# Spacing loads and transposes with small GpSimd reads, and moving reciprocals and row fetches, in an attention + gated-MLP kernel

## The chip, the cores and the metric

One core of one Trainium2 chip. The metric is device time in microseconds (us) of one launch, taken over several runs. Four compute engines matter: TensorE (PE in the profile), VectorE (DVE), ScalarE (ACT) and GpSimd (POOL). In these kernels SyncE (SP) only issues transfers.

## The reference

Shortened:

```python
B, N, m, C = 4, 12416, 32, 128
scale = 1.0 / np.sqrt(C)
def mab(q, kv):                       # attention without projections
    s = scale * (q @ kv.transpose(0, 2, 1))
    a = np.exp(s - s.max(-1, keepdims=True))
    a /= a.sum(-1, keepdims=True) + 1e-09
    return a @ kv
h = mab(inducing, x)                  # 32 rows per batch: needs ALL of x of that batch
y = mab(x, h).reshape(B * N, C)       # 49664 tokens
gate = 1 / (1 + np.exp(-(y @ w_gate)))          # 128 -> 1536
out = (gate * (y @ w_val)) @ w_out              # 1536 -> 128
```

`h` of a batch needs the whole batch, so the kernel computes `h` of batch b+1 while it runs the MLP of batch b. The inputs arrive in float32 and the kernel works in float16.

## The kernel before

The MLP runs in 97 blocks of 512 tokens, 24 to a batch. A block has 12 chunks of 128 hidden units. ScalarE makes `T = tanh(gate/2)` from TensorE's product; VectorE makes `u = (T + 1) * value`; TensorE multiplies `u` with `w_out`. In some "shared" blocks GpSimd makes 3 of the 12 products, from a copy of the value that ScalarE leaves in SBUF, to relieve VectorE:

```python
SHARED = (3, 7, 11, 15, 19, 23)                  # of 24 blocks, from block 5 on
def v_mul_pool(v32, bi, j0, n):
    ...
        nc.gpsimd.tensor_tensor(out=t[:], in0=v, in1=Ts[...], op=ALU.mult)
        nc.gpsimd.tensor_tensor(out=u[:, jj, :], in0=t[:], in1=v, op=ALU.add)
```

All engines run in a written order. `PLAN` is a string of 97 words, one per block: `A` and `B` are VectorE's products of two and of one chunk, `G`/`W` ScalarE's, small letters the products with `w_out`, and `J` takes the next side job (pieces of the next batch's attention). Each `A` starts one of four steps, and `at(n, k, f)` emits `f` at step k of block n. A shared block has no step 0, so what is due there comes with step 1.

The token rows of the second attention (`rep`) are made for eight blocks at a time, by a chain that starts at block n:

```python
def rep_events(n, b, d):
    put(n, 1, "s2", b, d)                # scores, exp
    at(n + 1, 0, e2_dma, b, d)           # small transpose, SyncE
    at(n + 1, 3, s2_sum, b, d)           # row sums: a tree of five adds, GpSimd
    at(n + 2, 3, s2_rec, b, d)           # reciprocal, VectorE
    at(n + 2, 3, a2_mul, b, d, 0)        # normalise, GpSimd
    at(n + 2, 3, a2_mul, b, d, 1)
    at(n + 3, 0, a2_dma, b, d, 0)        # transpose back, SyncE
    at(n + 3, 1, a2_dma, b, d, 1)
    at(n + 3, 2, rep_put, b, d, 0)       # to a DRAM scratch
    at(n + 3, 3, rep_put, b, d, 1)
    at(n + 4, 0, rep_get, b, d, 0)       # fetch of the new rows, four replicas
    at(n + 4, 1, rep_get, b, d, 1)
```

The next batch comes in six quarters of 512 KB each (`load_x`, issued by GpSimd; the code calls them q, 0 to 5). Each is transposed by a big transfer (`xT_dma`, SyncE), scored (`s1`), its weights are transposed by a small transfer (`a1_dma`), and they multiply the rows (`h`):

```python
for b in range(B):
    n0 = b * BB                          # BB = 24
    rep_events(n0 + 2, b, 1); rep_events(n0 + 10, b, 2)
    ...
        if b == 0:
            loads = ((1, 0), (2, 0), (5, 0), (6, 0), (8, 0), (9, 0))
            s1s, s1t, fin = (5, 9, 12), 6, 16
            hs = ((8, 1), (9, 1), (12, 2), (13, 1), (14, 3), (15, 1))
        else:
            loads = ((-10, 0), (-7, 0), (-4, 0), (-1, 0), (2, 0), (5, 0))
            ...
        for q, ((ln, lk), (hn, hk)) in enumerate(zip(loads, hs)):
            at(n0 + ln, lk, load_x, nb, q)
            at(n0 + ln + 1, 2, xT_dma, nb, q)
            put(n0 + hn, hk, "h", nb, q)
        ...
        rep_events(n0 + fin + 2, nb, 0)
```

The softmax here doesn't subtract the row's maximum and nothing guards it: scores larger than these inputs give would overflow.

## Time and profile before

| | us |
|---|---|
| three runs | 705.4, 706.2, 712.2 |
| profiled run | 715.1 (counted slow; span 713.3) |
| VectorE busy / idle of the span | 666.2 / 47.1 |
| ScalarE busy, TensorE busy, GpSimd busy | 662.5, 679.8, 309.6 |

The profiled run is over 1% longer than most runs, so it shows more stalls than the typical one; it is read for what the stalls are, not for how long the kernel takes.

Table of 20-us windows of the kernel before. Columns: stretch, its length, then busy us of TensorE, its weight loads, VectorE, ScalarE and GpSimd (with counts), granted TensorE clock, transfer engines' busy share, GB/s.

```profile
60.00:80.00 20.00, 19.52 (x114) 6.38 (x112) 19.99 (x24) 19.80 (x25) 11.43 (x15) 1.00 0.93 140
80.00:100.00 20.00, 16.35 (x97) 4.92 (x95) 13.62 (x17) 13.51 (x16) 4.60 (x6) 0.83 1.16 135
100.00:120.00 20.00, 14.15 (x97) 4.27 (x94) 12.24 (x15) 11.97 (x15) 3.80 (x5) 0.83 1.23 146
120.00:140.00 20.00, 19.91 (x142) 6.69 (x135) 19.86 (x25) 19.92 (x24) 12.76 (x17) 1.00 0.92 148
```

The first and last line are the normal state: VectorE and ScalarE both full (19.86 to 19.99 and 19.80 to 19.92 of 20 us), so that a hole in VectorE is lost time. The middle two lines are the two stalls, 14.1 us of VectorE idle, with the granted clock at 0.83 on average: in each of them it stood at half for 6.8 us.

The chain that ended last, before, in order of time (start, us, what): the three transfers that make up most of the stalls.

```profile
72.21 7.99 DMA a2T_1_1_1204<-a_0_1_1_1149
...
81.07 3.56 DMA rep_1_1278<-dt_1_0_1230
...
97.39 13.17 DMA xT_154<-xq_3_1283
```

The first two belong to the chain of `rep` for block 8; the third is a big transpose, which ran beside the load of quarter 4 (issued at 87.5 us, landed at 106.0).

### The profile page before, as it was taken

Reading aid. Unit: us, or ns where it says so; the run is one execution under the profiler, and the core shown is the slowest. Engines: PE = TensorE matmul, PEld = TensorE weight load, DVE = VectorE, ACT = ScalarE, POOL = GpSimd, SP = SyncE. Lnnn points to the kernel's source line nnn. Section 1 sums busy time; section 2 is a strip of 40 time slices with the busy share of each in tenths; the row PEclk is TensorE's granted clock in tenths of the full one; section 3 lists DMA queues with packets and bytes.
Section 4 is the critical chain, followed back from the end, with each engine's and each line's share of the span. In section 5 each row is a group of like instructions: output and inputs, shape, how many; then the busy total and the mean of one; then the engine's idle time right before and its main releaser. Section 6 shows DMA issues by size and latency. Waiting matters only on the chain.

```text
span 713.3 us, 13070 instructions
## 1 busy us (share of the span) xinstructions
PE 679.8 (95%) x4561; PEld 238.2 (33%) x4561; DVE 666.2 (93%) x792; ACT 662.5 (93%) x773; POOL 309.6 (43%) x389
## 2 busy tenths in 40 slices
PE   7899788999999999999999999999999999999997
PEld 4433222333333323333333333333333333333334
DVE  2599686999999999999999999999999999999997
ACT  4699776999999999999999999999999999999995
POOL 5234504452643541743541651634723534633423
PEclk9999898999999999999999999999999999999999
DMA  9599999884888792397688584454192353263222
GB/s 177 95 110 158 183 71 187 139 184 84 145 188 130 125 209 60 90 183 135 106 187 148 111 164 103 94 142 77 39 169 67 60 149 80 60 150 74 60 53 75
DMA packets 163955, 85.95 MB, mean 120 GB/s; under 512 B 133392, under 2 KB 148144, under 8 KB 163888
## 3 DMA queue, kind: packets, MB, share of 16 engines
q1 hardware_dynamic: 143904, 45.95, 38.2%
q0 software_dynamic: 19696, 39.03, 27.1%
q8 instruction: 35, 0.57, 0.4%
q14 instruction: 32, 0.26, 0.2%
q10 hardware_dynamic: 288, 0.13, 0.1%
HBM read 39.34 MB, written 28.31 MB: 95 GB/s over the span
## 4 chain that ended last, share of the span: by engine, by line
PE 64%; ACT 10%; DVE 9%; DMA 8%; issue 4%; POOL 3%; SPq 1%; DVEq 0%; ACTq 0%; POOLq 0%
DMA xq_4_132<-in_x_dram 2%; DMA xT_154<-xq_3_1283 2%; DMA a2T_1_1_1204<-a_0_1_1_1149 1%; SPq L397 1%; DMA a1n_2_3819<-e_2_2_3703 1%; DMA on_7763<-oT_7761 1%; DMA a1n_2_6256<-e_3_2_6162 1%; DMA on_5277<-oT_5275 1%; PE acc_1687 L538 1%; DMA rep_1_1278<-dt_1_0_1230 0%; PE acc_4267 L538 0%; PE acc_2641 L538 0%; PE acc_1770 L538 0%; PE acc_5765 L538 0%; PE acc_3334 L538 0%
## 5 line engine op out<-in xcount | busy, mean ns | idle before, releaser
L538 PEld LDWEIGHTS <-wo_117 128*128 128x128 f16 x1152 | 94.2, 98 | 147.7 <-issue 93.8
L428 PEld LDWEIGHTS <-hw_165 32*128 32x128 f16 x466 | 19.1, 91 | 59.9 <-issue 54.5
L428 PEld LDWEIGHTS <-hw_168 32*128 32x128 f16 x456 | 19.8, 91 | 56.2 <-issue 53.9
L428 PEld LDWEIGHTS <-hw_167 32*128 32x128 f16 x464 | 19.4, 91 | 54.1 <-issue 51.2
L428 PEld LDWEIGHTS <-hw_166 32*128 32x128 f16 x468 | 19.4, 91 | 52.4 <-issue 49.8
L428 PEld LDWEIGHTS <-hwp_172 128*128 128x128 f16 x120 | 11.7, 97 | 14.3 <-issue 4.7
L428 PEld LDWEIGHTS <-hwp_169 128*128 128x128 f16 x110 | 10.7, 98 | 15.8 <-issue 8.6
L428 PEld LDWEIGHTS <-hwp_171 128*128 128x128 f16 x112 | 10.9, 97 | 13.7 <-issue 5.8
L428 PEld LDWEIGHTS <-hwp_170 128*128 128x128 f16 x108 | 10.5, 97 | 14.6 <-issue 7.3
L566 POOL DMA_DIRECT2D out_dram<-on_1411 x1 | 0.5, 532 | 21.3 <-DMA on_1411<-oT_1409 21.3
L245 PEld LDWEIGHTS <-ones 128*128 128x128 f16 x96 | 6.9, 97 | 8.1 <-DMA a1n_2_6256<-e_3_2_6162 2.1
L190 PE MATMUL warm<-ones 128*128 128x512 f16 x16 | 5.6, 530 | 1.5 <-DVE ones L140 1.5
L767 PE MATMUL s_1_1657<-xT_154,indT 128*32 128x512 f16 x8 | 1.2, 605 | 5.8 <-DMA xT_154<-xq_2_1174 4.2
L495 DVE SCALAR_TENSOR_TENSOR u_8_1670<-T_4_1559,vb_2_1668 128x512 f16<-128x512 f16 x1 | 0.7, 690 | 6.4 <-PE vb_2_1668 L428 6.4
L214 ACT ACTIVATE e_1_2_1666<-s_1_1657 128x1024 f16<-128x1024 f32 x1 | 1.0, 1024 | 5.9 <-PE s_1_1657 L767 5.9
L310 POOL COPY hwp_169<-hw_165 32x128 f16<-32x128 f16 x2 | 0.6, 282 | 12.9 <-ACT hw_165 L303 12.8
L239 ACT ACTIVATE a1nt_205<-s1t_203 128x32 f16<-128x32 f32 x1 | 0.2, 198 | 6.0 <-PE s1t_203 L235 6.0
L495 DVE SCALAR_TENSOR_TENSOR u_4_1402<-T_2_1358,va_1_1399 128x1024 f16<-128x1024 f16 x1 | 1.2, 1222 | 4.2 <-PE va_1_1399 L428 4.2
L566 POOL DMA_DIRECT2D out_dram<-on_888 x1 | 0.5, 537 | 10.5 <-DMA on_888<-oT_886 10.5
L508 POOL TENSOR_TENSOR vt_0_6656<-v_59_2_6653,T_0_6643 128x512 f32<-128x512 f32 x1 | 1.1, 1150 | 8.3 <-PE s_2_6670 L324 8.3
L551 ACT ACTIVATE o_10374<-acc_10278 128x256 f32<-128x256 f32 x2 | 0.8, 384 | 4.3 <-PE acc_10278 L528 3.8
L482 ACT ACTIVATE T_0_1397<-g_0_1394 128x1024 f16<-128x1024 f32 x1 | 1.0, 1024 | 3.9 <-PE va_1_1399 L428 3.9
(4281 smaller groups left out, 2802.5 us busy)
## 6 DMA issues: line engine op xcount, KB each, us to landing
xq_0_120<-in_x_dram POOLq DMA_DIRECT2D x1, 512.0 KB, 5.1
xq_1_122<-in_x_dram POOLq DMA_DIRECT2D x1, 512.0 KB, 6.9
xq_2_128<-in_x_dram POOLq DMA_DIRECT2D x1, 512.0 KB, 8.3
xq_3_130<-in_x_dram POOLq DMA_DIRECT2D x1, 512.0 KB, 10.2
xq_4_132<-in_x_dram POOLq DMA_DIRECT2D x1, 512.0 KB, 13.4
xq_5_134<-in_x_dram POOLq DMA_DIRECT2D x2, 256.0 KB, 14.1
xq_0_770<-in_x_dram POOLq DMA_DIRECT2D x1, 512.0 KB, 6.2
xq_1_875<-in_x_dram POOLq DMA_DIRECT2D x1, 512.0 KB, 10.1
```

The lines of the kernel that those rows point to most:

```text
L190: nc.tensor.matmul(ps[:, 0:TOK], ones[:, 0:P], ones[:], start=True, stop=True)
L214: nc.scalar.activation(out=e1[:, 0:w], in_=ps[:, 0:w], func=AF.Exp, scale=SCALE)
L245: nc.tensor.matmul(ps[:, cs:cs + P], ones[:, 0:P], a1n[(b, q)][:, j, :], start=first and j == 0, stop=last and j == 3,)
L397: nc.sync.dma_start(rep[g * M:(g + 1) * M, 4 * i:4 * i + 4].rearrange("m r j t -> m r (j t)"), dt[:].rearrange("(r m) t -> m r t", m=M),)
L428: nc.tensor.matmul(ps[:, ds(col, TOK)], weights(k["b"]), rep[rows, 4 * k["i"] + k["r"]], start=True, stop=True,)
L482: nc.scalar.activation(out=Ts[(bi, p)][:, :, 0:T], in_=ps[:].rearrange("p (a t) -> p a t", a=2)[:, :, 0:T], func=AF.Tanh, scale=0.5,)
L495: nc.vector.scalar_tensor_tensor(out=u[:, :, 0:T], in0=Ts[(bi, j0 // 2)][:, j0 % 2:j0 % 2 + n, 0:T], scalar=1.0, in1=ps[:].rearrange("p (a ...
L508: nc.gpsimd.tensor_tensor(out=t[:], in0=v, in1=Ts[(bi, j0 // 2)][:, j0 % 2 + jj, :], op=ALU.mult)
L538: nc.tensor.matmul(accs[bi][:, 0:T], wo16[:, j, :], u, start=(c == 0), stop=(c == NJ - 1))
L551: nc.scalar.activation(out=o32[:, h:h + w, :].rearrange("p b c -> p (b c)"), in_=accs[bi][:, ds(h * P, w * P)], func=AF.Copy, scale=0.5,)
L566: nc.gpsimd.dma_start(out[ds(row0, QT)].rearrange("(p j) c -> p j c", j=QT // P)[:, 4 * k["r"]:4 * k["r"] + 4, :], on[:],)
L767: nc.tensor.matmul(ps[r * M:(r + 1) * M, ts(i, TOK)], indT[:], xTs[a[0]][:, ds(q * QT + r * TOK, TOK)], start=True, stop=True,)
```

## The change

Intent: a load and a big transpose should not be in flight together. A small GpSimd copy reads two columns of the transposed quarter q-1, so it waits for that transpose; it stands ahead of the load of quarter q. The loads of batch 1 are spread out, the chain of `rep` starts a block earlier with its later parts moved, stores come about half a block later, and the whole `PLAN` is redrawn for the new places.

```diff
 PLAN = (
-    "GAGBWGAabGBcGAfeGBdGAhBWgJ AGilkjBGGAabcBGAfGBedGAhGgBiG ...
+    "GAGBWGAabGBcGAfeGBdGAhBWgJG AilkjBGAJaBbGAcGBfeGAdWBhgG ...
     [all 97 words redrawn, cut]
+    def load_fence(b, q):
+        t = smp.tile([P, 2], F16, tag="fence", name=f"fence_{b}_{q}")
+        nc.gpsimd.tensor_copy(out=t[:], in_=xTs[b][:, ds(q * QT, 2)])
     def rep_events(n, b, d):
         put(n, 1, "s2", b, d)
         at(n + 1, 0, e2_dma, b, d)
-        at(n + 1, 3, s2_sum, b, d)
-        at(n + 2, 3, s2_rec, b, d)
-        [a2_mul at (n+2, 3); a2_dma at (n+3, 0) and (n+3, 1);
-         rep_put at (n+3, 2) and (n+3, 3); rep_get at (n+4, 0) and (n+4, 1), cut]
+        at(n + 2, 0, s2_sum, b, d)
+        at(n + 3, 0, s2_rec, b, d)
+        for i in range(2):
+            at(n + 3, 0, a2_mul, b, d, i)
+            at(n + 3, 1, a2_dma, b, d, i)
+            at(n + 3, 3, rep_put, b, d, i)
+            at(n + 4, 2, rep_get, b, d, i)
...
-        rep_events(n0 + 2, b, 1)
-        rep_events(n0 + 10, b, 2)
+        rep_events(n0 + 1, b, 1)
+        rep_events(n0 + 9, b, 2)
...
-                loads = ((1, 0), (2, 0), (5, 0), (6, 0), (8, 0), (9, 0))
-                s1s, s1t, fin = (5, 9, 12), 6, 16
-                hs = ((8, 1), (9, 1), (12, 2), (13, 1), (14, 3), (15, 1))
+                loads = ((0, 3), (2, 2), (4, 1), (6, 0), (7, 3), (9, 2))
+                s1s, s1t, fin = ((5, 1), (9, 0), (12, 1)), 6, 15
+                hs = ((7, 1), (7, 3), (11, 1), (11, 3), (14, 1), (14, 3))
+                wait = 4
+                [wait = 6 for the later batches, cut]
...
+                if q:
+                    at(n0 + ln, lk, load_fence, nb, q - 1)
                 at(n0 + ln, lk, load_x, nb, q)
-                at(n0 + ln + 1, 2, xT_dma, nb, q)
+                at(n0 + ln + (lk + wait) // 4, (lk + wait) % 4, xT_dma, nb, q)
...
-                at(n0 + sn + 1, 1, a1_dma, nb, [2 * e, 2 * e + 1])
+                at(n0 + sn + 1, 0, a1_dma, nb, [2 * e, 2 * e + 1])
...
-        if stores and (done_out[n] == 10 or n >= NBK - 2):
+        while stores and (n >= NBK - 2 or len(stores) > 1 and done_out[n] == 4):
             stores.popleft()()
```

More of the change, by code (lines that the diff above doesn't have):

```diff
@@ L25 @@
 PLAN = (
-    "GAGBWGAabGBcGAfeGBdGAhBWgJ AGilkjBGGAabcBGAfGBedGAhGgBiG AlkjBGGAbacBGAfWBedGAhJBgG "
-    "AilkjBGGAabcBGAfWBedGAhGgBiG AlkjBGGAbaBcWAGfeBGdAGBhGg AGilkBjGAJBabcAGefBGdAGhgBGi "
-    "AGlBkjJAGBaGbAGcGBefGAdhGBgG AikljBGGAbBaefGAdGBchG AgGBikGAljBJAGaBGbcGAGfBedG "
-    "AhGgBiGAlJBkGAjJBGAGbacBfeG AGdhBgiAGlkjBGGAbBJaAGcfBGe AGdhBGgAGiBkljGAGBabef "
-    "AGdBJcGAhgBGikAGljJBGAGbaBcfG AGedBGgAGhBilGAGkjBJAGBaGbcG AefGBdGAhgGBiGAkljBJAGbaGBcf "
-    "AGeGdBhGAgiWBlGAkjJBG AGabfBecGAGdBghGAikGBlJjAGBaGbcG AfGBedGAhJBgGAilkjBGGAabBcefG "
@@ L32 @@
-    "AdGBghGAilkjBGGAbaBGcGAfBJe AGdhBGgAGilBkjGAGBabef AGdcBGgGAhiBkljGAGBbacfAGedgGBhG "
-    "AilkjBGGAbacBWAGfBedGAhGgBiG AlkjBGGAbacBJAGfBGeAGdghBG AGilBkjGAGBbafeAGdcGBG "
-    "AghBGiAGklBJjAGGBbacfAGedBGg AGhiBGkAGljBJAGBGabcGAeGfBdG AgGhBiGAlGkBjGAJbaBcAGfeBGdh "
-    "AGgiGBkGAljBJAGbGBGa AGBefdGAGchBgGAiGBlkjGAGBabce AGfBJdAGhgBWiAGkBljGAGBbacf "
-    "AGedGBghAGilkjBGGAabBGcAGefBGd AGhgBGiAGlkjBJGABbGafG AedGBcGAhgBWiGAklBjJGAaGbBcG "
-    "AfeGBdGAhJBgGAilkjBGGAbacBfe AGdgGBhGAilkjBGGAaBJbAGceBGf AGdhBGgAGilkBjGAGBabef "
@@ L38 @@
-    "AGdcGBgGAhiBGkAGljBJAGBGbaceG AGfBdghGAiWBklGAjJBGAGabcBfG AGedBhGAgGBGAGilkJjBGAaGbBGcf "
-    "AGedBWhAGgilBkjGAJaBbG AceGBfGAdhBWgGAilBkjGAJbBaG AcfGBeGAdBWghAGilkBjGGAabBceG "
-    "AfGdBgGAhiBGGAlkjBGGAbacGBe AGfdBhGAGgilBkjAGGBbafe AGcdBGhAGgiBlkjGAGBabceAGfdBgG "
-    "AGhikBljGAGBabcGAefBGdAGhgBGi AGlBkjGAGaBbcGAJBfeGAdGBhgG AilkjBGGAabfBedGAcGBhgG "
-    "AikljBJGAbGBacGAfWBedAGhgGBiG AlkGBGAjBJAGbBGacGAfGBedG AhGgBiGAlGkBjGAGBbacfAGeBJd "
-    "AGghBGiAGlkjBJGABbaGfG AedBchGGAgiBkljGAGBabceGAfBdGgh AGikljBGAJBbaGAcWBfeGAdGhBgG "
@@ L44 @@
-    "AilkjBGAGabBcGAeGBGAGfdBGh AGgikBGAGlBjJAGBbGae AGfdBGhGAgciBGAGlkBjJGABbGacG "
-    "AfGeBdGAhgWBiGAkljBJAGbacBfG AeGBdGAhJBgGAilkjBGGAbacBfGG AedBghiGAlkjBGGAbaBfedG "
-    "AGhBgciAGlkBjJGAaBbGcfAGedWBhgG AiGlBkGAjJBGAGabBcWAGfBedG AGhgBiGAlGkBjJAGBbaGGcAGfBJe "
-    "AGdBGhgGAilkBjGAGbBafeG AdcGBgGAhiGBkGAljBJGAbacBfG AeGBdhGAgGiBlGAkjBWGAabBcefG "
-    "AdGBghGAilkjBGGAbacBfeGAGBdGh AGgilBkjGAGBefbaAGdgBWh AGicBkljGAGBbacGAefdBGAGghBiG "
-    "AGlkjBGAGBbacGAfeBWdAGhgBGi AGlBkjGAGBabcGAefGBdGAhGBgiG AkljBGGAfeBbadGAhWBgcG "
@@ L50 @@
-    "AilkBjGGAabBcGAfeGBdGAhgBGiG AlkBjGGAbaBcAGfWBedGAhgGBiG AlkjBJAGbacBGAfGeBGAdWBhgG "
-    "AikljBGGAfedBabGAGhBgiG AclkjBGGAabcBGAGfBedGAhWgBiG AGlkBjGAGBbacAGefBWAGdhgBG "
-    "AGiBlkjGAGBabcAGefBdJAGGhBgG AikGlBjGAGBabfeAGdgBWh AGciBkljGAGBabcGAefBGdAGhgiBG "
-    "AGkljBGAGBbacGAfeBWdGAhgBGi AGlBkjGAGBabcGAefGBdGAJBhgG AilkjBGGAfeBbadGAGhgBcG "
-    "AilBkjGGAabBcGAfBGedGAhgWiBG AlkjBGGAbacBGAGfeBdGAGBhgiG AlkjBGGAabcBGAGfeBdGAGBGhg "
-    "AGiBlkjGAGBefabAGdhBWgG AicBlkjGAGBbacGAefBGdAGhgBGi AGlkBjGAGBbacGAefBWdGAhgBGi "
@@ L56 @@
-    "AGlBkjGAGBbacGAefGBdGAhGgBiG AlkjBGGAfebBadGAgWBhcG AikBljGGAabBcGAfeGBdGAhGBgiG "
-    "AlkBjGGAbBacAGfBWedAGhgBGiG AlkBjGAGbaBcGAefBGdGAhGgBiG AlkjBGGAbafBeGAdWBhgG "
-    "AcikBljGABaGbAcfeBdAhgBilkj"
+    "GAGBWGAabGBcGAfeGBdGAhBWgJG AilkjBGAJaBbGAcGBfeGAdWBhgG AilkBjGGAbaBcGAfeGBdGAhgGBiG "
+    "AlkBjGGAbBacGAfWBedGAhGBgiG AlkjBGGAbaBWcAGfeBGdAGhBgG AGilBkjGAJaBbcAGfeBGdAGhgBGi "
+    "AGlkBjJAGBGabAGcGBefGAdhGBgG AikBJGAlBGjJAGBGbac AGefBGdGAhgBWiAGlkjBGAGBbace "
+    "AGfdBhGGAgilBkjGAJaBbcAGeBJfG AdgBGhAGilBkjGAGBabcfAGeGdBhG AgiJBGAGklBjJAGBWabeG "
@@ new lines @@
+    "AfdGBchGAgiGBkljAGBWabcAGefBJ AGdhBgGAGilBkjGAGBbacfAGedBGg AGhiBGlAGkjBJGABaGbGAGceBJ "
+    "AGBfGdgGAhiGBlJkjAGBGabfG AedBGcGAgBJhAGilkjBGGAbaBcfG AeGdBhGAgJBiGAlkjBWGAabcBeG "
+    "AGfBdhGAgGiBlGAkBGjGAGBabcf AGedBGhAGgikBljGAGBabefd AGhgGBcGAilkjBGGAabcBefGAdGBhgG "
+    "AikljBGGAbacBGAfWBedGAhgGBiG AlkjBGGAbacBJAGBfedGAGhBGg AGilkBjGAGBbafeAGdgWBhG "
+    "AicBGAGklBJjGAGBabcfGAedGBgG AhiBJAGkljBJGABaGbcGAfGBedG AghGBiGAlkBjGGAbaBcfGAGBeGd "
+    "AGhgiBkGAGljBJAGBWfeb AGaBGdhgAGicGBlGAkjBWGAabBcfG AeGBdgGAhJBiGAlkjBWGAabcBeG "
@@ new lines @@
+    "AGfdBhGAgGBilGAkGBjGAGBbacf AGedBGhgAGiBkljGGAbBaefG AdhGBgGAciGBlkAGjJBGAGabBcJ "
+    "AGBJefGAdhGBgGAilkjBGAJaBbG AcGfeBGAdGgBGhAGilBkjAGGBabcG AeGfBdGAghGBiGAlkBjWG "
+    "AfebBGadAGhgiBcGAGlkBjJAGBbGac AGfeGBdGAhgBGiAGkljBJGABaGbcG "
+    "AfedBhGGAgilBkjJAGBbacGGefAGdhBGg AGilkBjGAJaBbGAfWBed AGchGBgGAilkjBGAJbBaGAcWBfeG "
+    "AdGhBgGAikljBGGAabcBfGAeGBdG AhGgBiGAlkjBGGAbaBcfGAGBeGd AGhgBGiAGlkjBGAGBfeba "
+    "AGdgGBhGAiclBkjGAGBbacfAGedGBgh AGilkjBGGAabcBGAfWBedGAhGgBiG AlkjBGGAbaBcJAGfBedGAGhBGg "
@@ new lines @@
+    "AGiBlkjGAGBabfeAGdBWgh AGicGBlGAkjJBGAaGBbGAceBGfG AdBJhAGgiBGlAGkjBJAGBGbacG "
+    "AeGfBdGAhgGBiGAkGlBjGAGBbacf AGedBGgAGhiBGkAGljBJ AGBGabfeGAGdhBgcAGikljBGGAabBcfG "
+    "AeGBdhGAgJBiGAlkjBWGAabcBfG AGedBhGAgGiBlGAkGBjGAGBabcf AGedBGhGAgikBljGAGBabef "
+    "AGdgBGhGAciBJAGklGjBJAGBGbacG AefGBdhAGgJBiGAlkBjJAGbaceBG AfGdBhGAgGikBGAGBljGAGBabcG "
+    "AeGBfdGAhgGBiGAkljBWG AfeabBdhGAGgBiclGAkjBJGAbaBWceG AfdGBgGAhiGBlGAkjJBGAGbacBefG "
+    "AGBdghGAilGBkJjAGBbGacGAGefdBhG AgGBilGAkjBJGAbaBWe AGfdcBGAGgBhiGAGlBkjGAJBab "
@@ new lines @@
+    "AGcfeBGAGdhgBGAGikBljAGGBabc AGefBGdAGgBhiGAGkljBGAGBbacG AfGBedGAhGgBiGAlkjBWG "
+    "AfeBbadGAGBhgiGAclkjBGGAbacBfeG AdGBhgGAilkjBGGAbacBfGAeGBdG AhGgBiGAlkjBGGAbaBceGAGBfGd "
+    "AGhBgGiAGlkjBGAGBfeba AGdgBGhGAicBGkAGljBWAGBbacf AGeBGdgGAhiBGlGAkjBJGAabcBfG "
+    "AeGdBgGAhiGBlGAkjGBGAabBGc AGefBGdAGgBGhAGilkBjG AGBabfedGAhGBgcGAikljBGGAabBcefG "
+    "AdGhBgGAilkjBGGAabcBeGAfGBdhG AgGBiGAlkjBJGAbaGBGAGcBfeG AdGhBGgAGilkBjGAGBbaef "
+    "AGdcgBGGAhikBljGAGBabceAGfdhBGG AgikBljGAJaBbGAcfBWeAGdgBGh AGiklBjGAGBabcGAefBGdGAhgGBiG "
@@ L59 @@
+    "AlkjBGGAfebBadGAgWBhiG AclGBkjGAGBbacAGfeBWAGdhBgG AGiBlkjAGGBabcAGefBGdAGhgiBG "
+    "AGlkBjGAGBbacAGfBWeGAdgBGh AGiBlkjGAGBabfGAeBdcgG AGhiBkljGAGBabcAGefBWAGdBhgiG "
+    "AlkjBGGAbaBcGAfWBedGAhGgBiG AlkBjGAbGBaGAcGBfeGAGdhgBiG AklBjGGAabfBedGAhgBWcG "
+    "AilBkjGAGBabcGAefGBdGAhgBGiG AlkBjGAGbBacGAeWBfdAGhgGBiG AlkjBGAGbBacGAefBGdGAhGgBiG "
+    "AlkjBGGAbaBfedGAhWBgiG AclBkjAaBbcGGAfedBAhgiBlkj"
 )
@@ L693, in rep_events @@
         at(n + 1, 0, e2_dma, b, d)
-        at(n + 1, 3, s2_sum, b, d)
-        at(n + 2, 3, s2_rec, b, d)
-        at(n + 2, 3, a2_mul, b, d, 0)
-        at(n + 2, 3, a2_mul, b, d, 1)
-        at(n + 3, 0, a2_dma, b, d, 0)
-        at(n + 3, 1, a2_dma, b, d, 1)
-        at(n + 3, 2, rep_put, b, d, 0)
-        at(n + 3, 3, rep_put, b, d, 1)
-        at(n + 4, 0, rep_get, b, d, 0)
-        at(n + 4, 1, rep_get, b, d, 1)
+        at(n + 2, 0, s2_sum, b, d)
[5 more added lines that the diff above has]
+            at(n + 4, 2, rep_get, b, d, i)
     def m_mul():
@@ L734 @@
             if b == 0:
-                loads = ((1, 0), (2, 0), (5, 0), (6, 0), (8, 0), (9, 0))
-                s1s, s1t, fin = (5, 9, 12), 6, 16
-                hs = ((8, 1), (9, 1), (12, 2), (13, 1), (14, 3), (15, 1))
+                loads = ((0, 3), (2, 2), (4, 1), (6, 0), (7, 3), (9, 2))
+                s1s, s1t, fin = ((5, 1), (9, 0), (12, 1)), 6, 15
+                hs = ((7, 1), (7, 3), (11, 1), (11, 3), (14, 1), (14, 3))
+                wait = 4
             else:
                 loads = ((-10, 0), (-7, 0), (-4, 0), (-1, 0), (2, 0), (5, 0))
-                s1s, s1t, fin = (-2, 5, 9), 0, 14
-                hs = ((1, 1), (3, 1), (7, 1), (8, 1), (12, 1), (13, 1))
+                s1s, s1t, fin = ((-2, 1), (5, 1), (9, 1)), 0, 14
+                hs = ((1, 1), (3, 1), (8, 1), (8, 3), (12, 1), (13, 1))
+                wait = 6
             for q, ((ln, lk), (hn, hk)) in enumerate(zip(loads, hs)):
+                if q:
+                    at(n0 + ln, lk, load_fence, nb, q - 1)
                 at(n0 + ln, lk, load_x, nb, q)
-                at(n0 + ln + 1, 2, xT_dma, nb, q)
+                at(n0 + ln + (lk + wait) // 4, (lk + wait) % 4, xT_dma, nb, q)
                 put(n0 + hn, hk, "h", nb, q)
             at(n0 + loads[1][0], 1, load_tail, nb)
-            at(n0 + loads[1][0] + 1, 3, xTt_dma, nb)
-            for e, sn in enumerate(s1s):
-                put(n0 + sn, 1, "s1", nb, [2 * e, 2 * e + 1])
-                at(n0 + sn + 1, 1, a1_dma, nb, [2 * e, 2 * e + 1])
+            at(n0 + loads[1][0] + 2, 1, xTt_dma, nb)
+            for e, (sn, sk) in enumerate(s1s):
+                put(n0 + sn, sk, "s1", nb, [2 * e, 2 * e + 1])
+                at(n0 + sn + 1, 0, a1_dma, nb, [2 * e, 2 * e + 1])
             put(n0 + s1t, 1, "s1t", nb)
```

## The prediction

> **What bounds the kernel.** From about 60 us on, VectorE and ScalarE share the limit: the table of 20-us windows has both at 19.5 to 20.0 us of 20 nearly everywhere; a block takes about 6.8 us. Time can only come from holes in that stream. VectorE is idle 47.1 of 713.3 us; 22.4 of it lies before 60 us and about 5 in the last store, and both stay. Some 20 us remain, in few places: 14.1 us between 80 and 120 us (two stalls), 1.3 at 260, 1.2 at 375, 1.5 at 430.
>
> **The two stalls.** The chain of waits gives 72 to 85 us to the small transpose a2T (8.0 us), its copy, and rep_1 (3.6 us), the rows that block 8 waits for; and 97 to 110.6 us to the big transpose xT of quarter 3 (13.2 us). Both ran beside 512-KB loads: quarters 2 and 3 were issued 1.1 us apart at 67.3 us, quarter 4 at 87.5 us took 18.5 us to land. In later batches, alone, a big transpose lands in 4.3 to 5.8 us and a load in 6 to 8. [...] With each stall TensorE's clock was granted at half for 6.8 us, so 4 us of waiting cost 6 to 8.
>
> **What the change does.** Counts of operations are equal on every engine, except 15 GpSimd copies of 128x2 (an estimate of 0.2 us each, from the 128x32 add at 0.24 us): 3 us on an engine that is 43% busy. Each waits for a quarter's big transpose before the next load is issued, so they no longer overlap. The loads of batch 1 are spread at 1.75 blocks (12 us) instead of in pairs. The second rows are fetched at block 5 1/2 instead of 6: their reciprocals come later within the chain, but the chain starts a block earlier. Stores go about half a block later, so GpSimd stops waiting on their transposes (21.3 us once). The order of TensorE, VectorE and ScalarE work is redrawn around this; no work is saved.
>
> **On the critical path.** I expect both early stalls to go, with 1 to 2 us left (12 to 13 us gained in the profiled run), and some 2 of the later 5.7 us. The profiled run, at 715.1 us, should become about 699. But the timed runs before are 705.4, 706.2 and 712.2: stalls depend on how transfers happen to meet, and the profiled run had more than the typical one, which has only about 9 us to lose. Prediction: **699.0 us, range 694.5 to 704.0**. Faster by over 2% (below 692) would need more holes than there are: 0.06; within 2%: 0.92; slower: 0.02.
>
> **What would show it right.** No stretch after 60 us with VectorE below 18.5 of 20 us; granted clock 1.0 from 80 to 120 us; transposes xT of batch 1 landing in 4 to 7 us, not 9.7 median, its loads in 6 to 9; the waits for rep_1 and xT gone from TensorE's list; GpSimd's long waits at output stores replaced by short ones at the new copies; timed runs within 2 us. Wrong: a stall of similar size elsewhere in the first two batches.
>
> **What would make it wrong.** GpSimd works in order: a copy that waits for a late transpose also holds back the products for a2T and the shared value blocks, and could make a new stall near blocks 4 to 10. If the typical run before had hardly any stall, the gain shrinks to 2 to 3 us. The redrawn order may cost or win a few us, which counts don't tell.

## More of the kernel before

One reciprocal of the kernel before, with the GpSimd work ahead of it. Timeline: start us, us, engine, line, operation, out<-in.

```profile
233.98 1.27 POOL L511 TENSOR_TENSOR x_2_3407<-vt_2_3408,v_27_1_3405 128x512 f16<-128x512 f32 x1
...
235.81 1.16 POOL L353 TENSOR_TENSOR tree_1_1_3542<-e2n_1_3473 128x512 f32<-128x512 f16 x1
...
238.75 0.24 POOL L353 TENSOR_TENSOR rs_1_3541<-tree_1_1_3548 128x32 f32<-128x32 f32 x1
```

```profile
238.16 1.22 DVE L495 SCALAR_TENSOR_TENSOR u_0_3581<-T_0_3490,va_0_3578 128x1024 f16<-128x1024 f16 x1
...
243.41 0.34 DVE L361 RECIPROCAL rc_1_3650<-rs_1_3541 128x32 f32<-128x32 f32 x1
```

GpSimd finishes the last shared product at 235.3 us, then the sums at 239.0. VectorE starts block 28 at 238.16 (`u_0`) and meets the reciprocal at 243.41. The sums had been ready for 4.4 us.

## The result

| | before | after |
|---|---|---|
| median, us | 705.8 | 738.8 |
| lowest to highest (4 runs each) | 705.4 to 712.2 | 736.4 to 740.3 |

The ratio of after to before is 1.044, 95% interval 1.038 to 1.051: slower by 4.4%. A ratio here is the mean time of one kernel's fast runs over that of the other's fast runs of the same rounds, so it is not quite the ratio of the medians quoted. No run of either kernel comes near the other's.

Busy time hardly changed (VectorE 668.2 us after against 666.2, GpSimd 311.3 against 309.6). The time is in waits. What VectorE waited for, after (us in total, times, longest), the nine longest inside the blocks:

```profile
DVE hacc_158 L274 <- PE h_1417 L268: 6.1, 1, 6.1
DVE rc_1_3586 L366 <- POOL rs_1_3487 L358: 2.8, 1, 2.8
DVE rc_2_6852 L366 <- POOL rs_2_6771 L358: 2.7, 1, 2.7
DVE rc_2_9163 L366 <- POOL rs_2_9084 L358: 2.7, 1, 2.7
DVE rc_0_2771 L366 <- POOL rs_0_2689 L358: 2.6, 1, 2.6
DVE rc_2_4402 L366 <- POOL rs_2_4321 L358: 2.4, 1, 2.4
DVE rc_1_6032 L366 <- POOL rs_1_5935 L358: 2.4, 1, 2.4
DVE rc_1_8399 L366 <- POOL rs_1_8318 L358: 2.2, 1, 2.2
DVE rc_2_1943 L366 <- POOL rs_2_1824 L358: 1.6, 1, 1.6
```

Eight of the eleven reciprocals now wait for GpSimd's sums, 19.4 us in sum. The list of before has no such line. The place is the same one as shown above, block 28 (timeline, GpSimd then VectorE then TensorE; the bracket gives the idle time ahead and what ended it):

```profile
237.42 1.27 POOL L516 TENSOR_TENSOR x_2_3462<-vt_2_3463,v_27_1_3460 128x512 f16<-128x512 f32 x1
238.65 1.15 POOL L358 TENSOR_TENSOR tree_1_1_3488<-e2n_1_3382 128x512 f32<-128x512 f16 x1
...
241.58 0.24 POOL L358 TENSOR_TENSOR rs_1_3487<-tree_1_1_3494 128x32 f32<-128x32 f32 x1
```

```profile
238.33 0.68 DVE L500 SCALAR_TENSOR_TENSOR u_9_3575<-T_4_3505,vb_3_3573 128x512 f16<-128x512 f16 x1
241.85 0.35 DVE L366 RECIPROCAL rc_1_3586<-rs_1_3487 128x32 f32<-128x32 f32 x1 [2.83 <-POOL rs_1_3487 L358]
242.12 1.16 DVE L500 SCALAR_TENSOR_TENSOR u_0_3595<-T_0_3529,va_0_3592 128x1024 f16<-128x1024 f16 x1
```

```profile
243.33 0.61 PE L433 MATMUL va_1_3620<-rep_0_2931,hw_166 32*128 32x512 f16 x2 [2.79 <-DVE u_0_3595 L500]
```

The reciprocal now stands ahead of `u_0` of block 28, where before it stood ahead of `u_10`, 5.25 us later in that profile (238.16 to 243.41). In the redrawn order the shared products also end later against the block: 0.3 us ahead of VectorE's end of block 27 (238.69 against 239.0) where it was 2.9 us ahead of the start of block 28 (235.25 against 238.16), and the sums behind them 2.0 us later. So here 5.25 us plus 2.0 less 4.4 us of slack leave the wait of 2.8 us. VectorE stands with all its other products behind the reciprocal, in the written order: `u_0` starts at 242.12 us, 0.27 us after its start. TensorE stands too, 2.79 us in the last line, because no product frees its accumulators before `u_0`.

Block 28 is not typical in this. Over the eight places the sums of the kernel before end 0.8 to 4.7 us after the start of the block's first product, 20.3 us in all: an estimate, from that trace alone, of what a reciprocal ahead of that product would have waited. 19.4 us were measured. In sum the early place alone explains the waits; later sums as at block 28 are made up by earlier ones elsewhere. (A ninth reciprocal, in block 4, moved likewise; its sums end 10 us earlier in the changed kernel, and it does not wait.)

The clock added to each of the eight stands. Windows after, same columns as before: the first early stall, then two of the eight stands.

```profile
76.00:96.00 20.00, 13.92 (x104) 4.60 (x102) 12.42 (x16) 11.45 (x14) 9.76 (x12) 0.83 0.97 175
116.00:136.00 20.00, 18.36 (x133) 6.11 (x132) 16.48 (x21) 16.39 (x19) 10.94 (x15) 0.91 0.66 138
235.00:252.00 17.00, 14.16 (x83) 4.11 (x79) 11.96 (x16) 12.25 (x14) 10.16 (x15) 0.80 0.66 109
```

A direct wait of 2.83 us cost VectorE 5.0 us in the last of these lines (17.00 less 11.96), because matmuls of 512 columns took 0.61 us afterwards (the first at 243.33 us) and not 0.39. Over the eight stretches that hold the stands VectorE is idle 31.2 us: 19.4 us of direct waits and 11.8 us more. Experiment 3 shows what this more depends on. The clock records of this trace have a half-clock stretch (granted share 0.50) at each of the eight, 3.4 us long seven times and 6.8 us once; TensorE's gaps there are 1.5 to 2.8 us long (see the last section).

The ninth loss is the early one, 7.6 us of VectorE at 76 to 96 us: TensorE waited 5.9 us for the small transpose `a1n` that its first product of batch 1 reads.

What the change wanted, it got: the loads of batch 1 land in 5.5 to 6.9 us (before 6.2 to 18.5) and its big transposes in 4.3 to 6.0 us (before 4.3 to 21.1). The price was on GpSimd, which stood at one of the new copies (its timeline, after):

```profile
77.96 0.18 POOL L138 COPY fence_2_1292<-xT_154 128x2 f16<-128x2 f16 x1 [13.92 <-DMA xT_154<-xq_2_1117]
```

### The profile page after: what moved, and what is told of

Same layout as the page of the kernel before. It is cut to its first block, busy times and chain, and to the rows that moved or that the text cites. A ratio compares the mean times of both kernels' runs of the same rounds, so it can differ in the third digit from the quotient of the medians.

```text
span 736.5 us, 13077 instructions
## 1 busy us (share of the span) xinstructions
PE 690.9 (94%) x4561; PEld 238.3 (32%) x4561; DVE 668.2 (91%) x792; ACT 663.8 (90%) x773; POOL 311.3 (42%) x404
## 5 line engine op out<-in xcount | busy, mean ns | idle before, releaser
L433 PEld LDWEIGHTS <-hw_166 32*128 32x128 f16 x464 | 18.5, 91 | 61.9 <-issue 59.8
L513 POOL TENSOR_TENSOR vt_0_9392<-v_87_2_9389,T_0_9373 128x512 f32<-128x512 f32 x1 | 1.2, 1151 | 14.4 <-ACT v_87_2_9389 L839 14.4
L513 POOL TENSOR_TENSOR vt_0_10091<-v_95_2_10088,T_0_10078 128x512 f32<-128x512 f32 x1 | 1.2, 1151 | 12.3 <-PE va_2_10110 L433 12.3
L513 POOL TENSOR_TENSOR vt_0_9746<-v_91_2_9743,T_0_9731 128x512 f32<-128x512 f32 x1 | 1.2, 1152 | 12.0 <-PE va_2_9762 L433 12.0
L138 POOL COPY fence_2_1292<-xT_154 128x2 f16<-128x2 f16 x1 | 0.2, 184 | 13.9 <-DMA xT_154<-xq_2_1117 13.9
L513 POOL TENSOR_TENSOR vt_0_4261<-v_35_2_4258,T_0_4248 128x512 f32<-128x512 f32 x1 | 1.2, 1151 | 10.9 <-PE acc_4200 L543 10.9
L513 POOL TENSOR_TENSOR vt_0_2192<-v_15_2_2189,T_0_2178 128x512 f32<-128x512 f32 x1 | 1.2, 1152 | 10.8 <-ACT v_15_2_2189 L839 10.8
L513 POOL TENSOR_TENSOR vt_0_9017<-v_83_2_9014,T_0_9004 128x512 f32<-128x512 f32 x1 | 1.2, 1152 | 10.8 <-ACT v_83_2_9014 L839 10.8
```

The lines of the kernel that those rows point to most:

```text
L138: nc.gpsimd.tensor_copy(out=t[:], in_=xTs[b][:, ds(q * QT, 2)])
L433: nc.tensor.matmul(ps[:, ds(col, TOK)], weights(k["b"]), rep[rows, 4 * k["i"] + k["r"]], start=True, stop=True,)
L513: nc.gpsimd.tensor_tensor(out=t[:], in0=v, in1=Ts[(bi, j0 // 2)][:, j0 % 2 + jj, :], op=ALU.mult)
```

## The experiments

Theory A: the reciprocal stands too early for sums that GpSimd makes behind the shared products, and eight stands with the half clock after them are the loss. Rival B: the new copies hold GpSimd back, and the late sums are only their shadow. Rival C: the redrawn order of TensorE work costs the time. Each group of runs was on one chip with its own runs of the kernel before, whose times are given beside it. In listings of some runs the names carry no buffer numbers.

### 1. The reciprocals half a block later

```diff
-        at(n + 3, 0, s2_rec, b, d)
+        at(n + 3, 2, s2_rec, b, d)
         for i in range(2):
-            at(n + 3, 0, a2_mul, b, d, i)
-            at(n + 3, 1, a2_dma, b, d, i)
-            at(n + 3, 3, rep_put, b, d, i)
-            at(n + 4, 2, rep_get, b, d, i)
+            at(n + 3, 2, a2_mul, b, d, i)
+            at(n + 3, 3, a2_dma, b, d, i)
+            at(n + 4, 1, rep_put, b, d, i)
+            at(n + 4, 3, rep_get, b, d, i)
```

> The changed kernel with the reciprocals and the products after them half a block later (step 2 of block n+3 instead of step 0), their transposes, copies and fetches one or two quarter steps later. Theory A (in the changed kernel VectorE stands at a reciprocal 1.6 to 2.8 us, eight times, because GpSimd does the sums after the nine-us pile of shared products, and each stand costs 3 to 4.5 us with the half clock after it): the eight waits vanish, about 30 us are gained, 705 to 713 us; the stall at 80 us stays. Rival B (the new GpSimd copies hold GpSimd back): little change, 730 to 739. Rival C (the redrawn order of TensorE work costs the time): little change too.

Measured: 706.6 us (704.5 to 707.4), before on this chip 706.9 (702.5 to 711.2), ratio 1.000 (0.996 to 1.004). No wait for the sums is left. The early window, and then the one in which the changed kernel lost 3.5 us of VectorE at a reciprocal:

```profile
76.00:96.00 20.00, 13.77 (x106) 4.73 (x105) 12.81 (x16) 11.89 (x14) 9.76 (x12) 0.83 1.02 168
116.00:136.00 20.00, 19.86 (x151) 6.86 (x149) 19.83 (x25) 19.28 (x24) 11.15 (x15) 1.00 0.80 135
```

Two steps' place of the reciprocal, and of what follows it, give back 32 us of the 33 us lost (738.8 less 706.6, on different chips; 31.2 us were read from the windows). `PLAN` and the copies are those of the changed kernel, so neither is slow by itself: rival C falls, and B as the cause of this loss. The early stall is untouched.

### 2. The sums half a block earlier, the reciprocals where they are

```diff
-        at(n + 2, 0, s2_sum, b, d)
+        at(n + 1, 2, s2_sum, b, d)
```

> The changed kernel with the sums (the GpSimd tree) half a block earlier, so that they stand between the two groups of shared products instead of behind both; the reciprocals stay where they are. Theory A: each wait of VectorE shrinks by the 2.4 us of the second group, from 1.6 to 2.8 us to 0 to 0.5, and most of the 30 us come back: 705 to 720 us. Rivals B and C: no change, 730 to 739.

Measured: 717.4 us (716.9 to 718.6), ratio to before 1.016 (1.011 to 1.021), on the chip of experiment 1. The eight stands are gone (one wait of 0.2 us at a reciprocal is left), which is A from the other side, with the reciprocal's followers left where the change put them. The rest of the gain to 706 went elsewhere: the sums now delay shared products, for which TensorE waited 4.8 us in three places, and the early stall grew to 11.5 us of VectorE between 75 and 100 us. GpSimd had no room there; moving the reader was better than moving the sums.

### 3. The changed kernel without the copies

```diff
-                if q:
-                    at(n0 + ln, lk, load_fence, nb, q - 1)
```

> The changed kernel without the 15 GpSimd copies, nothing else changed. Theory A: the eight waits at reciprocals stay at about 2 us each, 728 to 740 us; only the stall near 80 us may change, by up to 7 us, since GpSimd stood 13.9 us at the third copy there. Rival B (the copies hold GpSimd back): the waits shrink and the time falls to 700 to 712.

Measured: 736.6 us (734.7 to 742.9), same chip, ratio to before 1.045 (1.038 to 1.051). VectorE's waits for the sums, in total, times, longest:

```profile
DVE rc L366 <- POOL rs L358: 23.4, 9, 3.6
```

They stayed and one more came. B is wrong as the cause.

This trace also tells what a stand costs. The same reciprocal waits 2.4 us and TensorE 2.25 us in the changed kernel and here, but here no half clock follows (windows, changed kernel, then this run; the granted clock is third from the end):

```profile
290.00:315.00 25.00, 22.74 (x137) 7.19 (x138) 21.31 (x26) 21.26 (x26) 14.86 (x18) 0.93 0.51 90
290.00:315.00 25.00, 22.74 (x145) 7.64 (x144) 22.23 (x27) 22.44 (x27) 14.33 (x17) 1.00 0.59 89
```

VectorE is idle 3.7 us with the half clock and 2.8 us without. From 3 us before each wait to 11 us after the reciprocal's start, VectorE lost 0.9 to 2.2 us beyond the wait at the eight stands of the changed kernel, and 0.1 to 0.4 us at the four stands that no half clock followed (two here, two in experiment 5).

### 4. The kernel before, again

> The kernel before, unchanged, for one more profile. If it falls in a run of 705 us, the two stalls between 80 and 120 us should be smaller than in the profile at hand (14.1 us of VectorE idle there): about 5 us. If it is 712 to 715 us again, the same two stalls.

Measured: 710.2 us, one run, state unknown. It is neither of the two cases that were expected. Between 80 and 120 us VectorE lost only some 2 us, but it lost 6 us between 250 and 265 us, where TensorE waited 2.7 us for an `a1n`, and 3 us near 420 us, where it waited 1.7 us for another. So the stalls of the kernel before move from run to run; that its scatter (702.5 to 711.2 us on this chip) is what its transfers happen to meet is an estimate, from these two profiles. It has no wait for the sums either.

### 5. The reciprocal early, in the kernel before

```diff
-        at(n + 2, 3, s2_rec, b, d)
+        at(n + 1, 3, s2_rec, b, d)
```

> The kernel before with one word changed: the reciprocal stands at once behind the GpSimd sums it reads (step 3 of block n+1), one block earlier than before; nothing else of the change is in it. In the profile of before one set of sums ended at 239.0 us and its reciprocal ran at 243.4 us, so one block (6.8 us) earlier VectorE must stand about 2.4 us. Theory A: up to eleven such waits of 2 to 3.5 us, each followed by half clock, 4 us lost each: 735 to 755 us. If the change owes its loss to its order of TensorE work or to the GpSimd copies (rivals B and C), VectorE's early reciprocal alone costs no more than the waits: under 725.

Measured: 763.5 us (759.2 to 767.1), before on this chip 706.9 (699.8 to 717.8), ratio 1.082 (1.076 to 1.087).

```profile
DVE rc L361 <- POOL rs L353: 44.5, 11, 6.6
```

All eleven reciprocals wait, 4.0 us each on average. The direction is as A says; the size is above the range that was expected, since the waits were longer than the 2 to 3.5 us worked out from one slack. So the disease can be given to the kernel before with one number, and with nothing of the change in it. The dose is larger than the change's: a whole block, where the change moved the reciprocal by three steps, and all eleven reciprocals instead of nine. Three steps alone in the kernel before were not run; the 20.3 us above are the estimate for them.

### 6 and 7. What is left at 82 us: the early stall

In experiment 1 TensorE waits at 82 us. What it waits for, and SyncE's issue of it:

```profile
PE h L250 <- DMA a1n<-e: 6.1, 1, 6.1
```

```profile
72.98 1.98 SPq L198 DMA_TRANSPOSE xT<-xq  x1
75.05 4.24 SPq L402 DMA_DIRECT2D rep<-dt  x8
79.39 3.82 SPq L226 DMA_TRANSPOSE a1n<-e  x1
```

The transpose stands behind eight fetches, though its input was ready at 70.8 us, and it takes 8.5 us to land, beside the load that GpSimd issued at 78.0 us. Two remedies were tried on top of experiment 1. First, the product one block later:

```diff
 PLAN, blocks 7 and 8:
-AikBJGAlBGjJAGBGbac AGefBGdGAhgBWiAGlkjBGAGBbace
+AikBGAlBGjAGBGbac AGefBGdGAJhgBWiAGlkjBGAJGBbace
-                hs = ((7, 1), (7, 3), (11, 1), ...
+                hs = ((8, 1), (8, 3), (11, 1), ...
```

> rec_late with one more edit: the first two products of batch 1 (h of quarters 0 and 1) stand one block later in the order of TensorE work, in block 8 instead of block 7, as in the kernel before. In rec_late TensorE stood 6.1 us at 82 us for the small transpose a1n that the first of them reads, and with the half clock after it VectorE lost about 7.2 us between 80 and 95 us. If that wait is the whole of what is left, it goes and the time falls by 6 to 7 us to about 699 to 700 us. If the transfers are merely too slow there, another wait on the same stretch (the rows rep of block 8) takes its place: 703 to 707.

Measured: 703.8 us (702.5 to 704.9); before on this chip 704.3 (702.0 to 710.7), ratio 0.997 (0.993 to 1.002). The wait went, but only part of the gain came. Another wait took its place. It is neither the fetch of `rep` nor the transpose, but the copy (timeline, GpSimd, then ScalarE):

```profile
77.03 0.18 POOL L138 COPY fence<-xT 128x2 f16<-128x2 f16 x1 [10.22 <-DMA xT<-xq]
77.54 0.54 POOL L127 DMA_DIRECT2D xq<-in_x_dram  x1 [0.33 <-issue]
78.09 1.17 POOL L513 TENSOR_TENSOR vt<-v,T 128x512 f32<-128x512 f32 x1
```

```profile
81.87 3.77 ACT L487 ACTIVATE T<-g 128x1024 f16<-128x1024 f32 x4 [1.32 <-POOL vt L513]
```

The shared products of block 7 stood behind the copy and the load, ScalarE waited 1.3 us for one of them, and half clock for 6.8 us followed. Second remedy, also on top of experiment 1 alone, the transpose ahead of the fetches in SyncE's queue:

```diff
-                at(n0 + sn + 1, 0, a1_dma, nb, [2 * e, 2 * e + 1])
+                early = b == 0 and e == 0
+                at(n0 + sn + (not early), 2 * early, a1_dma, nb, [2 * e, 2 * e + 1])
```

> rec_late with the small transpose a1n of quarters 0 and 1 of batch 1 issued half a block earlier, ahead of the fetch of rep on the same queue (SyncE); the products stay in block 7. In rec_late it was issued at 79.4 us, 8.7 us after its input was ready, behind eight fetches, and beside the load issued at 78.0 us. If the place in the queue is what made it late, most of the 6.1 us go: 699 to 702 us. If the contention of transfers is, it stays above 704.

Measured: 705.6 us (703.3 to 706.3), ratio 0.999 (0.995 to 1.004), same chip. By the number alone that would speak for contention. Yet the profile shows that the early stall was cured by the earlier issue: the transpose went out at 74.1 us, ahead of the fetches, and landed in 3.5 us; VectorE lost 0.7 us between 80 and 85 us and hardly anything after it, where experiment 1 lost 7.2 between 76 and 96 us. In its place the next `a1n` (quarters 2 and 3) was waited for, 2.9 us at 110 us with half clock after it. The time alone would have misled. But queue and contention are not told apart: the earlier transpose also landed (77.7 us) just after the load of that time was issued (77.0 us), so it was out of that load's way, and the next `a1n`, issued at 103.8 us beside a load of 102.4 us, took 8.7 us to land. In experiment 1 the transpose lost on both counts: 8.6 us from input to issue, and 8.5 us instead of 3.5 from issue to landing.

### 8. Experiment 1 without the copies

Same edit as in experiment 3, on top of experiment 1.

> rec_late without the 15 GpSimd copies. If the copies do what they are meant for (a load never beside a big transpose), leaving them out brings early waits back: 2 to 8 us slower than rec_late, 708 to 714. If the spacing of the loads does it and the copies only cost: same or faster by up to 5 us, 701 to 706.

Measured: 711.3 us (705.4 to 714.7), ratio 1.007 (1.002 to 1.013), on the chip of 6 and 7. Against experiment 1 (1.000, 0.996 to 1.004, another chip) the intervals touch. It points to the copies being of use; see 11.

### 9. The kernel before with the load part alone

The copies and the new places of loads and big transposes, in the kernel before; its `PLAN`, its chain of `rep`, its stores.

> The kernel before with the load part of the change alone: the new places of loads and big transposes and the GpSimd copies; order of TensorE work, chain of the rows rep, reciprocals and stores as before. If the idea of taking turns is right, the early stalls of before shrink and it runs 2 to 5 us faster than before, 700 to 704 us; if the copies hold GpSimd back, slower than before.

Measured: 707.6 us (706.1 to 712.4), ratio 1.004 (0.999 to 1.009), same chip. No gain, contrary to the 700 to 704 us that were expected. Its profile has small losses at 80 to 105 us, but still the waits for `a1n` at 250 and 420 us, 3.5 us in two places. Taking turns, copies and new places of loads together, does not by itself make the kernel faster.

### 10. The whole put together

First (`best_a`), on top of `h_later`: the loads of quarters 3 to 5 of batch 1, and so the copies, behind the shared products.

```diff
-                loads = ((0, 3), (2, 2), (4, 1), (6, 0), (7, 3), (9, 2))
+                loads = ((0, 3), (2, 2), (4, 1), (6, 3), (8, 2), (10, 1))
```

> h_later with the loads of quarters 3, 4 and 5 of batch 1 (and with them the GpSimd copies and the big transposes) half to three quarters of a block later, so that the copy that stood 10.2 us in h_later stands behind the shared products of block 7, not ahead of them. If the copy that holds GpSimd back caused what is left near 82 us (ScalarE waited 1.3 us for such a product, half clock for 6.8 us, about 4 us lost), the time falls to 698 to 701 us. If not, 703 to 705.

Then (`best_b`), on top of it, the small transposes of quarters 0 to 3 earlier:

```diff
-                at(n0 + sn + 1, 0, a1_dma, nb, [2 * e, 2 * e + 1])
+                early = {0: (5, 2), 1: (9, 3)}.get(e) if b == 0 else None
+                at(*(early or (n0 + sn + 1, 0)), a1_dma, nb, [2 * e, 2 * e + 1])
```

> best_a with the two small transposes a1n of quarters 0 to 3 of batch 1 issued half and a quarter block earlier, as in a1_first. Removes what waits for a1n are left in the first two batches: equal to best_a within 1 us if best_a has none, up to 3 us faster if it has one. Expected 698 to 701 us.

Measured, on one chip: `best_a` 702.2 us (701.4 to 703.5), ratio 0.995 (0.992 to 0.999); `best_b` 701.4 us (701.3 to 702.2), ratio 0.994 (0.991 to 0.997). The kernel before ran at 706.9 (699.8 to 717.8) there. In `best_b` GpSimd meets the third copy after the products and does not wait at it, and the window of the early stall has full clock:

```profile
80.98 1.27 POOL L516 TENSOR_TENSOR x<-vt,v 128x512 f16<-128x512 f32 x1
82.19 0.60 POOL L571 DMA_DIRECT2D out_dram<-on  x1
82.79 0.20 POOL L138 COPY fence<-xT 128x2 f16<-128x2 f16 x1
82.91 0.54 POOL L127 DMA_DIRECT2D xq<-in_x_dram  x1
```

```profile
76.00:96.00 20.00, 18.08 (x135) 6.40 (x135) 18.22 (x23) 17.01 (x21) 9.33 (x13) 1.00 0.89 162
```

The next two copies stand 9.8 and 8.9 us, and no engine waits long for what is behind them (the longest wait for GpSimd in the list is 0.3 us): these two stands of GpSimd cost nothing by themselves.

`best_b` is faster than the kernel before by 0.6%, with an interval that excludes 1 but well inside the 2% that count as the same, and its six runs lie within 0.9 us where the ten fast runs of the kernel before scatter over 7.7 (699.8 to 707.5; two more, at 712.3 and 717.8, are counted slow). The kernel before has single runs that are faster (699.8). So this version is worth steadiness more than speed. Both were expected at 698 to 701 and missed that by a little: 1.8 us of VectorE remain idle in this window of `best_b`, with no long wait in the list.

### 11. The same without the copies

> best_b without the 15 GpSimd copies, all else equal. If the copies are what keeps the runs of best_b together (701.3 to 702.2 us, where the kernel before scatters from 699.8 to 717.8), the median rises by 2 to 6 us and the scatter of runs to over 4 us, as rec_late without them scattered from 705.4 to 714.7. If the spacing of the loads and the new places of the small transposes do it, the runs stay at 700 to 702.5 us and within 2 us.

Measured: 708.8 us (702.5 to 710.7), before on that chip 708.1 (699.8 to 713.4), ratio 1.004 (0.997 to 1.012). That is another chip than that of `best_b`. The ratios to before differ by a hundredth and their intervals touch only at the edge (0.9911 to 0.9974 and 0.9969 to 1.0116); the scatter grew from 0.9 to 8.1 us. Its profile shows the expected collision: the largest landing of a big transpose is 12.9 us, not 6.8 (that transpose was issued at 44.5 us, 0.2 us ahead of a load), and the median of the loads 7.6 us, not 6.3. That the copies keep loads and big transposes apart is thus shown in the traces. That this saves time, when the rest of the kernel leaves the copies room, is what experiments 8 and 11 both point to, each with its two kernels on two chips and with intervals that meet.

## Why the prediction was wrong

- **The limit** was read rightly: VectorE and ScalarE full, time only in holes. That cuts both ways. The prediction counted the holes that could be filled and not the slack that could be used up.
- **The step that failed** is the one about the rows: "their reciprocals come later within the chain, but the chain starts a block earlier". Both halves are true. Their sum, a reciprocal three steps earlier in the block, was used only to say when the rows would be fetched. It was never set against the sums the reciprocal reads, although the trace before has them: at the eight places ready 0.5 to 4.4 us ahead, where three steps are 5.25 to 5.8 us. That the sums fall behind the shared products in the shared blocks could have been read from the order of the changed kernel's GpSimd work. Measured: eight waits, 19.4 us, which with their half clock are 31.2 us.
- **"no work is saved"** and "Counts of operations are equal on every engine" are right and say little. An order of work with equal counts was 4.4% slower.
- **"The redrawn order may cost or win a few us"** named the right place with a size wrong by a factor of ten. At block 28 the redrawn order did put the shared products some 2.6 us later against the block (0.3 us instead of 2.9), but over the eight places this evens out (20.3 us estimated with the old sums, 19.4 measured), and the order isn't slow of itself: with the reciprocals moved it runs like the kernel before (experiment 1).
- **"I expect both early stalls to go"**: the transfers did get faster, as predicted (loads 5.5 to 6.9 us, big transposes 4.3 to 6.0), and the waits for `rep` and `xT` left TensorE's list. But an early stall of 7.6 us stayed, with half clock from 85.8 to 92.6 us, at an `a1n` that the change had made due a block earlier, behind the fetches in SyncE's queue. This is close to the "stall of similar size elsewhere in the first two batches" that the prediction named as the sign of being wrong: the place is nearly the old one, the transfer another.
- **The danger named last**, that a copy waiting for a late transpose holds back the shared products near blocks 4 to 10, was real: 13.9 us of GpSimd standing there, and the wait that was left over in experiment 6. It was worth about 3.5 us (what VectorE lost from 76 to 96 us in experiment 6), not the 33.
- **"GpSimd's long waits at output stores replaced by short ones at the new copies"** was half wrong: the wait of 21.3 us went, but waits of up to 8.3 us at stores stayed, and the copies brought ones of up to 13.9 us.
- **The amount to be gained** (about 699 us) was near what could be had: the best version runs at 701.4 us.

What stays open: why `best_a` and `best_b` keep some 1.8 us of VectorE idle between 76 and 100 us, and how the remaining scatter of the kernel before divides among its transfers, since the profile shows another stall in each run. The stores' new place was never tested by itself. Nor is it known what exactly brings the half clock on (see the last section).

## What to carry to other kernels

When an instruction moves earlier in an engine's written order, look up when its inputs were ready before, not only whether it used to wait: the slack is invisible in a list of waits, and when it was used up here the whole engine stood, 1.6 to 2.8 us, behind one instruction of 0.35 us. On a full engine a wait can cost more than its length: here 31 us for 19 us of waiting, with TensorE's clock at half for 3.4 us (once 6.8) at each stand. A throttle on transfers such as the small copy belongs behind the urgent work of the engine that carries it, where here it seemed to pay; ahead of that work it moved the stall.

## What the traces show of the clock and of the transposes

- Half clock came with gaps of TensorE of 1.5, 1.8, 2.2, 2.2, 2.3, 2.4, 2.5 and 2.8 us at the eight reciprocals of the changed kernel: it began 0.3 to 1.8 us after the gap's end, and at two of them 0.3 and 0.5 us before it. But gap length does not decide: 1.5 and 1.6 us in the kernel before and 1.5 and 2.25 us in experiment 3 were not followed by it (granted clock 1.00), and experiment 6 had it with no gap over 1.1 us. Inside the kernels' blocks the half-clock stretches last 3.4, 6.8 or 10.2 us, once 13.7 (experiment 2). In the trace of the changed kernel they begin at 85.81, 126.77, 184.80, 242.83, 304.27, 416.91, 474.93, 587.57 and 645.60 us, each a whole multiple of 3.41 us (12 to 33 times) after the one before. This is read off the clock records; no run tested it.
- The 512-KB transposes of batch 1 landed in 4.3 to 6.0 us in the changed kernel, where no load of that batch ran beside them, and in up to 21.1 us in the kernel before, where loads did.
- The results were correct in every run, with the copies and without. The times differ: with the 15 copies that keep loads and big transposes apart left out of `best_b`, the largest landing was 12.9 us, not 6.8, and the scatter of six runs, on another chip, 8.1 us, not 0.9.
